# A fused sparse attention and gated convolution kernel: another order for its hand-scheduled operations

## The chip, the cores and the metric

The kernel runs on one core of one Trainium2 chip. The core has five engines that work through queues of their own: TensorE (PE; its weight loads are listed as PEld), VectorE (DVE), ScalarE (ACT), GpSimd (POOL) and SyncE (SP, which here only issues transfers). The metric is the device time of one execution in microseconds (us), lower is better.

## The reference

Four batches of eight heads, 768 positions, 64 wide. Attention keeps, for each query, only the six chunks of 32 keys with the highest upper bound; the result goes through a causal five-tap gate, a product with `w_val` and a product with `w_out`.

```python
ub = np.sum(np.maximum(q[..., None, :] * k_min, q[..., None, :] * k_max), axis=-1)
top_chunks = np.argsort(np.where(causal, ub, -1e9), axis=-1)[..., -6:]
scores = np.where(sel & (pos[:, None] >= pos[None, :]), scale * q @ k.T, -1e9)
attn = softmax(scores)
x = (attn @ v).transpose(0, 2, 1, 3).reshape(B, S, H * D)
gate = sigmoid(sum(conv_w[k] * xp[:, k:k + S, :] for k in range(5)))
out = (gate * (x @ w_val)) @ w_out
```

## The kernel before

The 32 heads are taken as 16 pairs, numbered 0 to 15; four pairs make a batch. `build` lists the operations, each with its engine and what it reads and writes; `emit_in_order` issues them in the order of the table `ORDER`. Each engine then works through its own operations in exactly that order and waits at the first whose inputs, buffer or PSUM bank is not ready. A name is a kind, a pair and indices; digits behind "=" are PSUM banks, of which there are eight, and a bank that an operation takes must have been read out by the users before it.

The kinds, for pair p:

- `Lk`, `Lq`, `Lv` (SP) load k, q and v. `KT`, `QT` (PE, L641) transpose them. `KE` (ACT, L648) and `QH` (ACT, L683) copy the transposes out, `QL` (DVE, L722) keeps the rounding rest of q. `KX` (DVE, L654) takes the maximum and minimum of each chunk of keys, and `KB`, `KS` (POOL, L664 to L679) turn these into operands.
- `CF`, `BD` (PE, L755, L766) make the bounds, `T8` and `CM` (DVE, L774, L781) select the chunks into `NS`. The mask has to be transposed to `QM`: by PE and DVE (`MT`, L791, and `ME`, L795) for pairs 0 to 9, by a DMA transpose (`MD`, SP, L797) for pairs 10 to 15.
- `S` (PE, L809 to L814) makes the scores, in six parts of two banks each, one bank for each head; the mask enters as a second product (L814). `E` (ACT, L818) is the exponential, `A` (POOL, L830) the causal cut, `AV` (PE, L839) the product with v, `RC` and `NR` (DVE, L845, L849) the division, into `ON`.
- `XT` transposes the result into `xT`: by PE and `XTE` (DVE, L871, L882), or by a DMA transpose (SP, L863) for pairs 8 to 14. `XH` (POOL, L890) copies the edge for the convolution. `CV` (PE, L903) is the gate for two pairs, `TH` (ACT, L908) its tanh.
- For each batch b, `VL` (PE, L918) multiplies with `w_val`, `GV` (DVE, L924) applies the gate, `OU` (PE, L932) multiplies with `w_out`, `OE` (ACT or DVE, L940, L942) copies out and `ST` (SP, L945) stores.

The weights come in small transfers: POOL issues `wval`(j, r), eight of them, and `wout`; SP then copies each finished pair of `wval` to the other half of the partitions (`wvd`j, L1026).

PE uses its array in three shapes: whole (128 rows, most kinds), in halves (64 rows, `S` and `VL`) and in quarters (32 rows, `CV`).

Of the kernel before, what the change touches and what calls it, by code (L numbers as in the profile page):

```python
# [126 lines left out]
S1.3=35 E1.13 E1.03 CF2=6 AL2 BD2.1 BD2.5 BD2.4 Lv0 VC0 QL3.1 A1.13 KX3.00 KX3.11 KX3.01 KB3.5 KB3.0
KB3.1 BD2.2 BD2.3 T82.2 T82.5 T82.1 T82.3 QH3.0 S1.1=07 E1.11 E1.01 Lq4.0 A1.01 S1.4=54 QL3.0 T82.4
CM2 AH3 E1.14 S1.0=31 E1.10 E1.00 E1.04 A0.15 Lv1 KS3 KB3.2 KB3.3 Lq5.0 KT4.1=7 KX4.11 AV0.05=2
AV0.03 AV0.02 A1.14 KT4.0=0 S1.2=64 E1.12 E1.02 MT2=1 AV0.01 AV0.14=3 AV0.15 KX4.00 KX4.10 KX4.01  # L130
KB4.5 KB3.4 ME2 QT4.1=5 AV0.04 AV0.00 RC0.0 AV0.13 AV0.10 AV0.11 QH4.1 NR0.0 KE4.1 KE4.0 Lk5.0
AV0.12 QT4.0=4 QH4.0 S2.3=61 E2.13 S2.2=27 E2.12 E2.03 AL3 CF3=0 BD3.5 BD3.4 BD3.2 BD3.1 KB4.0 KS4
# [12 lines left out]
XTE0 AV2.10 RC2.1 MT5=3 ME5 KT7.0=6 S4.1=07 E4.11 A3.04 A3.15 E4.01 S4.0=54 E4.00 E4.10 S5.3=32
NR2.1 A3.01 KX7.01 AH6 KX7.00 A3.05 AV3.02=1 A3.03 KB6.0 AV3.01 AV3.04 AV3.03 KB6.5 KS6 AV3.05 A3.14
AV3.00 wval31 wval01 E5.03 KT7.1=7 KX7.11 KX7.10 RC3.0 NR3.0 QT7.0=0 QH7.0 QL7.0 A4.05 A4.13 QT7.1=5
QH7.1 KE7.1 KE7.0 A3.13 AV3.14=4 AV3.15 Lv5 A4.14 XH1 KB6.1 KB6.2 KB6.4 KB6.3 A4.03 A4.04 A4.15
CF6=3 A4.01 BD6.3 QL7.1 BD6.1 AV3.10 AV3.11 AV3.13 E5.13 BD6.4 AV3.12 RC3.1 NR3.1 S5.1=17 E5.11 AH7
S5.5=06 E5.05 E5.15 BD6.2 BD6.5 E5.01 S5.4=25 E5.14 E5.04 dg00 T86.5 T86.1 T86.4 T86.3 KB7.0 S5.0=70  # L150
# [6 lines left out]
TH1.00 S6.4=32 TH1.10 TH1.11 E6.14 E6.04 XT4=0 XTE4 KT9.0=6 KX9.01 KX9.00 KT10.1=5 A5.13 A6.05
QT9.1=7 VC7 KB8.5 Lk12.0 QH9.1 MT7=4 ME7 QL9.1 KB8.0 A5.04 wval10 A5.11 QT9.0=0 QH9.0 QL9.0 XT3=2
XTE3 VC5 AV5.02=4 A5.01 TH1.01 KB8.1 A6.13 KE9.0 A6.03 KS8 AV5.04 Lv9 AV5.03 AV5.05 AV5.01 AV5.00
S7.5=37 E7.05 AL8 S7.3=10 E7.03 KX10.11 RC5.0 AL9 KX10.10 S7.1=62 E7.01 A6.11 KB8.2 KB8.3 AV5.14=3  # L160
AV5.12 AV5.15 E7.15 A6.14 wval20 AV5.13 AV5.11 E7.13 CF8=1 KB8.4 BD8.4 KE10.1 BD8.1 AV5.10 E7.11
NR5.0 A6.04 BD8.5 KB9.5 BD8.3 BD8.2 KB9.0 A7.01 A6.01 S7.2=67 E7.02 E7.12 T88.5 RC5.1 T88.3 T88.2
# [5 lines left out]
S8.3=72 E8.03 E8.13 E8.12 E8.10 A7.14 T89.4 T89.5 XT6=1 T89.3 T89.1 CM9 XTE6 XT5=5 XTE5 AV7.12=0
MT9=4 ME9 KB10.5 KT11.0=7 KX11.00 KX11.01 KT11.1=1 KS10 KE11.1 A7.05 A8.15 A8.14 A7.13 AV7.00=2
AV7.15 AV7.13 AV7.11 AV7.14 AV7.10 RC7.1 NR7.1 A7.04 AV7.02 AV7.05 KE11.0 KX11.11 KB10.1 KB10.2  # L170
AV7.04 dg11 KX11.10 AV7.03 AV7.01 RC7.0 NR7.0 KB10.4 S9.5=56 E9.05 E9.15 S9.3=43 S9.4=70 E9.03 E9.14
S9.1=56 E9.11 E9.13 CF10=4 KB10.3 BD10.3 VC8 A8.13 BD10.1 A8.11 BD10.2 BD10.4 BD10.5 E9.01 A9.15
AV8.14=1 E9.04 A8.03 T810.5 T810.2 dg13 KB11.0 KB11.5 KB11.1 AV8.13 AV8.11 AV8.12 A8.01 AV8.10
AV8.15 RC8.1 T810.3 Lq11.0 Lq12.0 QT11.1=0 QH11.1 T810.4 Lk13.0 Lv11 NR8.1 QL11.1 QT11.0=2 QH11.0
T810.1 KS11 A9.05 A9.13 A9.11 QL11.0 KT12.1=6 KE12.1 S9.2=35 E9.02 KX12.11 CM10 KX12.10 S9.0=71
E9.00 E9.12 E9.10 KT12.0=0 dg10 AL11 KX12.00 QT12.1=2 QH12.1 AH11 QL12.1 QT12.0=3 QH12.0 QL12.0
KE12.0 XH5 CV5.0=7456 CV5.1 TH5.11 TH5.00 TH5.01 TH5.10 A8.04 VC9 AV8.02=1 AV8.01 KB11.2 AV8.04
A8.05 KB11.3 KB11.4 XH3 CF11=2 BD11.4 A9.14 BD11.5 BD11.3 wvd2 wvd3 wvd0 MD10 S10.4=36 E10.14
KX12.01 T811.3 S10.5=07 BD11.2 T811.2 T811.5 AV8.05 E10.05 KB12.5 AV8.03 E10.04 S10.3=54 E10.03
# [918 lines left out]
```

## Time and profile before

| | |
|---|---|
| three runs, us | 183.22, 183.95, 182.49 (median 183.22) |
| profiled execution, us | 182.86, of it 181.2 span (first to last instruction) |
| busy, us | PE 175.2, PEld 127.3, ACT 140.4, DVE 123.3, POOL 109.1 |
| granted TensorE clock | 1.00 throughout |
| transfers | 29.68 MB, 28.06 MB of it on SP's queue |

A busy engine in the table counts each instruction from its start to its end, and the next may start before. Idle time and waits are named by what came last before the engine went on. A start in a timeline is in us from the start of the span.

### The profile page before, as it was taken

The page shows a single profiled execution, that of the slowest core. Times are in us where ns is not written, and L with a number is a line of the kernel's source. Part 1 is how long each engine was busy: PE and PEld are TensorE (multiplying, and loading weights), DVE is VectorE, ACT ScalarE, POOL GpSimd, SP SyncE. Part 2 cuts the span into 40 slices and gives each one's busy share as a digit, 9 for nine tenths or more (in the row PEclk, how much of TensorE's full clock was granted, in tenths as well). Part 3 has the DMA queues.
Part 4 walks back from the last instruction along what each step waited for, and adds up shares of the span by engine and source line. Part 5 has one row for each costly group of instructions (what it writes and reads, how often), then busy time and mean ns, then how long its engine had stood idle before and what let it go on. Part 6 is the DMA issues. An engine that isn't in the chain of part 4 may idle for free.

```text
span 181.2 us, 8892 instructions
## 1 busy us (share of the span) xinstructions
PE 175.2 (97%) x3714; PEld 127.3 (70%) x3714; DVE 123.3 (68%) x429; ACT 140.4 (78%) x320; POOL 109.1 (60%) x309
## 2 busy tenths in 40 slices
PE   7999999999999999999999999999999999999991
PEld 5896667868878687787866685687567678656541
DVE  0569999999999799998765679558925233611360
ACT  2279999999999999999897867595867979357032
POOL 6955898999999979899919633374551615000000
PEclk9999999999999999999999999999999999999999
DMA  5999999999999999980697995895226149337045
GB/s 99 224 220 215 213 201 236 213 211 227 210 222 190 219 191 189 183 175 10 135 164 150 207 206 117 176 95 149 43 47 103 60 117 231 96 108 289 7 183 222
DMA packets 89912, 29.68 MB, mean 164 GB/s; under 512 B 85387, under 2 KB 86667, under 8 KB 89872
## 3 DMA queue, kind: packets, MB, share of 16 engines
q1 hardware_dynamic: 88880, 28.06, 73.5%
q0 software_dynamic: 992, 1.06, 4.5%
q8 instruction: 29, 0.48, 1.2%
q14 instruction: 11, 0.09, 0.2%
HBM read 20.98 MB, written 6.29 MB: 151 GB/s over the span
## 4 chain that ended last, share of the span: by engine, by line
PE 91%; DVE 5%; issue 1%; POOL 0%; ACT 0%
PE ps L918 12%; PE ps L839 12%; PE ps L932 12%; PE ps L641 11%; PE ps L811 10%; PE ps L903 9%; PE ps L814 9%; PE ps L766 6%; PE ps L950 4%; DVE KK L654 2%; PE ps L871 2%; PE ps L791 2%; PE ps L809 2%; PE ps L714 1%; DVE ON L849 1%
## 5 line engine op out<-in xcount | busy, mean ns | idle before, releaser
L818 ACT ACTIVATE P<-ps 128x512 f16<-128x512 f32 (+1 forms) x192 | 90.2, 600 | 5.4 <-PE ps L814 4.8
L830 POOL TENSOR_SCALAR_AFFINE_SELECT P<-P 128x256 f16<-128x256 f16 (+1 forms) x128 | 43.1, 358 | 23.6 <-ACT P L818 21.9
L654 DVE TENSOR_REDUCE KK<-ps 128x12 f32<-128x384 f32 x64 | 32.8, 550 | 7.1 <-PE ps L641 6.5
L814 PE MATMUL ps<-QM,EM 64*128 64x512 f16 (+4 forms) x256 | 36.9, 290 | 0.2
L811 PE MATMUL ps<-QH,KE 64*128 64x512 f16 (+4 forms) x256 | 35.1, 291 | 0.0
L924 DVE SCALAR_TENSOR_TENSOR GV<-G,ps 128x384 f16<-128x384 f32 x32 | 16.4, 548 | 22.8 <-PE ps L918 22.1
L839 PEld LDWEIGHTS <-P 128*128 128x128 f16 x672 | 26.1, 98 | 6.3 <-issue 3.3
L839 PE MATMUL ps<-VA,P 128*128 128x65 f16 x672 | 30.3, 194 | 0.2 <-issue 0.2
L940 ACT ACTIVATE OSB<-ps 128x512 f32<-128x512 f32 (+1 forms) x22 | 12.9, 594 | 15.6 <-PE ps L932 8.4
L918 PE MATMUL ps<-xT,wv 64*128 64x384 f16 x256 | 23.3, 323 | 0.3 <-issue 0.3
L932 PE MATMUL ps<-wo,GV 128*128 128x512 f16 (+1 forms) x100 | 22.7, 370 | 0.0
L774 DVE MAX8 TOP<-ps 128x8 f32<-128x16 f32 (+4 forms) x160 | 15.9, 166 | 6.6 <-PE ps L766 5.1
L918 PEld LDWEIGHTS <-wv 64*128 64x128 f16 x256 | 13.1, 94 | 8.3 <-issue 1.2
L908 ACT ACTIVATE G<-ps 128x384 f32<-128x384 f32 x32 | 13.9, 498 | 6.6 <-PE ps L903 6.6
L811 PEld LDWEIGHTS <-KE 64*128 64x128 f16 x256 | 13.6, 94 | 6.2 <-issue 1.6
L849 DVE TENSOR_TENSOR ON<-ps,RCP 128x384 f16<-128x384 f32 x32 | 17.5, 552 | 0.7
L648 ACT ACTIVATE KE<-ps 128x384 f16<-128x384 f32 x32 | 17.0, 569 | 1.0 <-DVE RCP L845 0.7
L683 ACT ACTIVATE QH<-ps 128x384 f16<-128x384 f32 x32 | 16.0, 556 | 2.3 <-PE ps L641 2.2
L903 PE MATMUL ps<-xT,diag 32*32 32x384 f16 x1280 | 17.3, 326 | 0.0
L741 POOL CAST VA<-vn 128x768 f16<-128x768 f32 x16 | 14.6, 915 | 3.8 <-DMA vn<-in_v_dram 3.7
L641 PE MATMUL ps<-ident,kn 128*128 128x128 f32 x96 | 15.7, 284 | 0.0
L903 PEld LDWEIGHTS <-diag 32*32 32x32 f16 x1280 | 14.0, 87 | 2.5 <-ACT P L818 0.4
(75 smaller groups left out, 304.3 us busy)
## 6 DMA issues: line engine op xcount, KB each, us to landing
vn<-in_v_dram SPq DMA_DIRECT2D x16, 384.0 KB, 6.1
out_dram<-OSB SPq DMA_DIRECT2D x23, 256.0 KB, 2.9
kn<-in_k_dram SPq DMA_DIRECT2D x30, 192.0 KB, 5.0
qn<-in_q_dram SPq DMA_DIRECT2D x30, 192.0 KB, 4.8
wv<-in_moe_w_val_dram POOLq DMA_DIRECT2D x8, 64.0 KB, 4.5
wo<-in_moe_w_out_dram POOLq DMA_DIRECT2D x4, 128.0 KB, 5.3
wv<-wv SPq DMA_DIRECT2D x4, 128.0 KB, 5.1
qn<-in_q_dram SPq DMA_DIRECT2D x4, 96.0 KB, 3.1
```

Of the source, the lines that this page charges most:

```text
L641: nc.tensor.transpose(out=pt[:, tl * 128:(tl + 1) * 128], in_=t[:, 3 * w + tl, :], identity=ident)
L648: nc.scalar.activation(out=KE[p % 3][:, w * HB:(w + 1) * HB], in_=bank(gr, None), func=AF.Copy)
L654: nc.vector.tensor_reduce(out=KK[p % 2][:, mx, w * 12:(w + 1) * 12], in_=bank(gr, None).rearrange("p (c t) -> p c t", t=CH), axis=AX.X, op ...
L811: nc.tensor.matmul(out=pq[hh][:, col + a:col + n], lhsT=KE[p % 3][HP[hh], ks], rhs=QH[p % 3][HP[hh], q0 + a:q0 + n], start=True, stop=False)
L814: nc.tensor.matmul(out=pq[hh][:, col + a:col + n], lhsT=EM[HP[hh], ks], rhs=qm[HP[hh], q0 + a - 128:q0 + n - 128], start=False, stop=True)
L818: e.EX = lambda p, hh, bi, tot, gr: nc.scalar.activation(out=PT[hh, bi, p % 2][:, 0:tot], in_=bank(gr, None)[:, 0:tot], func=AF.Exp, scale ...
L830: nc.gpsimd.affine_select(out=ap, in_=ap, pattern=[[0, n], [1, 128]], compare_op=ALU.is_ge, fill=0.0, base=0, channel_multiplier=-1)
L839: nc.tensor.matmul(out=pav[:, qt, :], lhsT=PT[a, bi, p % 2][:, col:col + 128], rhs=VA[p % 3][:, hh, jt, :], start=(jt == 0), stop=(jt == qt))
L849: e.NR = lambda p, hh, gr: nc.vector.tensor_tensor(out=ON[(p // 2) % 2][:, 2 * (p % 2) + hh].rearrange("p t h d -> p h t d"), in0=bank(gr, ...
L903: nc.tensor.matmul(out=pc[i][os], lhsT=diag[rs, cp * NG + gi, j, :], rhs=x[rs, gi, :, a:a + 128], start=(j == 0), stop=(j == 2 * KSZ - 1), ...
L918: nc.tensor.matmul(out=pv[h], lhsT=wval_sb[HP[h], n, wc:wc + 255:2], rhs=xT[HP[h], (b % 2) * 2 + cp, gi, :, LD:LD + 128], start=(n == 0), ...
L932: nc.tensor.matmul(out=po[:, 0:z - a], lhsT=GVT[(b % 2) * NCT + et][:, s * 128:(s + 1) * 128], rhs=wout_sb[:, et, a:z], start=(et == 0), s ...
```

## The change

Only the table `ORDER` is other: the same 140 operations stand first, and after them the same operations as before stand in another order. 342 of PE's 564 operations have another place in PE's queue (by up to 25 places), 158 of ACT's 319, 223 of DVE's 347, and 254 of POOL's 294 (by up to 83 places). SP's queue is the same, row for row. Some operations take another PSUM bank. PE changes between the three shapes of its array 82 times in place of 79. The table has one line less, so that every line number behind it is lower by one.

```diff
-KE2.1 G8 S0.5=46 E0.05 KB1.0 KB1.5 KB1.1 KS1 KB1.2 KB1.3 S0.4=51 E0.14 E0.15 E0.04 Lq3.0 S0.3=27
+KE2.1 G8 S0.5=46 E0.05 KB1.0 KB1.5 KB1.1 KS1 KB1.2 KB1.3 S0.4=51 E0.14 E0.15 E0.04 dg01 KB1.4 dg03
...
-XT14 NR15.1 ST2.0 OE2.1 ST2.1 OE2.2 XT15=3 XTE15 CV13.0=0217 CV13.1 TH13.01 OU2.4=5 OE2.4 XH15
+TH13.11 OU2.3=3 OU2.4=5 OE2.3 OU1.3=6 OE1.3 OU1.4=4 OE1.4 NR14.0 XT14 XH15 CV15.0=1063 CV15.1
```

PE, pair 3, the score parts S3.4 and S3.1. `ps` are PSUM tiles, `VA` with `P` is an AV, `KB` with `RH` to `QL` a BD. Before, the first product of S3.1 (L809) follows S3.4 (L811, L814) directly:

```order
L811 MATMUL ps_1000<-QH_96,KE_86 128x512
L811 LDWEIGHTS KE_86
L811 MATMUL ps_1001<-QH_96,KE_86 128x512
L814 LDWEIGHTS EM
L814 MATMUL ps_1000<-QM_89,EM 128x512
L814 LDWEIGHTS EM
L814 MATMUL ps_1001<-QM_89,EM 128x512
L809 LDWEIGHTS KE_86
L809 MATMUL ps_1008<-QH_96,KE_86 128x192
```

Now two BD (six matmuls each, the last one shown) and two AV stand between them:

```order
L813 MATMUL ps_990<-QM_89,EM 128x512
...
L765 MATMUL ps_958<-KB_115,QL_99 128x48
...
L838 MATMUL ps_932<-VA_94,P_1_140 128x65
...
L765 MATMUL ps_958<-KB_115,QL_99 128x48
...
L838 MATMUL ps_932<-VA_94,P_1_140 128x65
...
L838 MATMUL ps_932<-VA_94,P_1_142 128x65
...
L808 MATMUL ps_1018<-QH_96,KE_86 128x192
```

Bounds of pair 4 (BD4.3, BD4.1) and products of pair 1 (AV1.10, AV1.11) have moved between the two score parts; PE changes its array's shape twice more here.

POOL, the transfers of `w_val` (`wv`). Before, wval31 and wval01 stand together, ahead of the first edge copy (XH1, the two copies of `xT`):

```order
L830 AFFINE_SELECT P_1_143<-P_1_143 128x128
L1023 DMA wv_66<-in_moe_w_val_dram 32x2x512 x2
L830 AFFINE_SELECT P_0_126<-P_0_126 128x128
L830 AFFINE_SELECT P_0_130<-P_0_130 128x256
L830 AFFINE_SELECT P_1_142<-P_1_142 128x256
L830 AFFINE_SELECT P_0_131<-P_0_131 128x128
L890 COPY xT<-xT 128x4x2x4
```

Now wval01 stands behind the second edge copy (XH5, the first two rows) and the four operations that follow it:

```order
L889 COPY xT<-xT 128x4x2x4
L889 COPY xT<-xT 64x4x4
L829 AFFINE_SELECT P_0_130<-P_0_130 128x256
L673 COPY KB_115<-KC_114 64x4x24
L829 AFFINE_SELECT P_0_132<-P_0_132 128x128
L829 AFFINE_SELECT P_0_125<-P_0_125 128x128
L1022 DMA wv_66<-in_moe_w_val_dram 32x2x512
```

wval01 has moved from among the cuts of pairs 3 and 4 to among those of pair 8; SP's queue still has wvd0, which copies what it brings, directly ahead of MD10.

DVE, the divisions (RC, NR) of pairs 14 and 15 and the copy XTE15. Before, both NR of pair 14 stand ahead of those of pair 15:

```order
L849 TENSOR_TENSOR ON_150<-ps_4844,RCP_147 128x2x3x64
L845 RECIPROCAL RCP_148<-ps_4892 128x6
L849 TENSOR_TENSOR ON_150<-ps_4830,RCP_147 128x2x3x64
L845 RECIPROCAL RCP_148<-ps_4858 128x6
L849 TENSOR_TENSOR ON_150<-ps_4858,RCP_148 128x2x3x64
L849 TENSOR_TENSOR ON_150<-ps_4892,RCP_148 128x2x3x64
L882 COPY xT<-ps_4968 128x6x128
```

Now NR14.0, the last one that the DMA transpose XT14 needs, stands behind XTE15:

```order
L848 TENSOR_TENSOR ON_150<-ps_4848,RCP_147 128x2x3x64
L844 RECIPROCAL RCP_148<-ps_4861 128x6
L848 TENSOR_TENSOR ON_150<-ps_4861,RCP_148 128x2x3x64
L844 RECIPROCAL RCP_147<-ps_4832 128x6
L844 RECIPROCAL RCP_148<-ps_4868 128x6
L848 TENSOR_TENSOR ON_150<-ps_4868,RCP_148 128x2x3x64
L881 COPY xT<-ps_4961 128x6x128
L848 TENSOR_TENSOR ON_150<-ps_4832,RCP_147 128x2x3x64
```

NR14.0 has moved behind three more operations of DVE, and XT14 with it.

## Rows read from the trace of the kernel before

**Rows 1.** Stretches: us, then busy us (instructions) by engine, clock, DMA share, GB/s.

```profile
40.00:60.00 20.00, 19.86 (x382) 15.77 (x381) 19.38 (x73) 19.94 (x48) 18.91 (x56) 1.00 1.13 213
60.00:80.00 20.00, 19.95 (x511) 16.20 (x513) 18.17 (x61) 19.39 (x44) 17.28 (x46) 1.00 1.02 197
80.00:100.00 20.00, 19.76 (x587) 14.12 (x580) 14.60 (x51) 17.98 (x43) 15.25 (x43) 1.00 0.59 117
100.00:120.00 20.00, 20.00 (x417) 14.20 (x413) 13.48 (x41) 14.53 (x34) 8.65 (x29) 1.00 0.82 169
```

**Rows 2.** The chain that ended last: start, us, what.

```profile
159.99 3.56 PE ps L932 x16
...
168.57 0.32 issue
```

**Rows 3.** Timeline of PE at a change of shape: start, us, engine, line, operation.

```profile
30.79 0.21 PE L766 MATMUL ps<-KB,QH 128*128 128x48 f16 x2
30.84 0.18 PE L766 MATMUL ps<-KB,QL 128*128 128x48 f16 x1
30.95 0.23 PE L811 MATMUL ps<-QH,KE 64*128 64x128 f16 x2
```

**Rows 4.** Timeline of PE, the two heads of S3.1.

```profile
36.47 0.24 PE L809 MATMUL ps<-QH,KE 64*128 64x192 f16 x1
...
36.71 0.24 PE L809 MATMUL ps<-QH,KE 64*128 64x192 f16 x1
```

**Rows 5.** Timelines of PE and DVE, 64.9 to 66.8 us: XT3, AV5, S7.1, XTE3.

```profile
64.91 0.50 PE L871 MATMUL ps<-identh,ON 128*128 128x128 f16 x6
65.45 0.84 PE L839 MATMUL ps<-VA,P 128*128 128x65 f16 x21
...
66.75 0.24 PE L809 MATMUL ps<-QH,KE 64*128 64x192 f16 x2
...
66.10 0.55 DVE L882 COPY xT<-ps 128x768 f16<-128x768 f16 x1
```

**Rows 6.** Issues on the page: median us from issue to landing at the end.

```profile
wv<-in_moe_w_val_dram POOLq DMA_DIRECT2D x8, 64.0 KB, 4.5
...
QM<-NS SPq DMA_TRANSPOSE x6, 2.6
```

**Rows 7.** Timelines of SP, DVE, POOL and PE, 76 to 90 us.

```profile
76.64 2.79 SPq L1026 DMA_DIRECT2D wv<-wv  x3
85.88 1.30 SPq L797 DMA_TRANSPOSE QM<-NS  x1
...
89.08 3.28 SPq L1026 DMA_DIRECT2D wv<-wv  x1
...
77.22 1.02 DVE L882 COPY xT<-ps 128x768 f16<-128x768 f16 x2
...
80.05 1.39 POOL L830 TENSOR_SCALAR_AFFINE_SELECT P<-P 128x256 f16<-128x256 f16 x4
...
89.19 0.39 PE L811 MATMUL ps<-QH,KE 64*128 64x512 f16 x2
```

**Rows 8.** Timelines of PE, DVE, SP and POOL, 155 to 164 us.

```profile
157.51 0.50 PE L871 MATMUL ps<-identh,ON 128*128 128x128 f16 x6
...
163.48 1.84 PE L903 MATMUL ps<-xT,diag 32*32 32x384 f16 x139
...
156.21 1.02 DVE L849 TENSOR_TENSOR ON<-ps,RCP 128x384 f16<-128x384 f32 x2
158.49 0.56 DVE L882 COPY xT<-ps 128x768 f16<-128x768 f16 x1 [1.25 <-PE ps L871]
...
155.79 1.39 SPq L863 DMA_TRANSPOSE xT<-ON  x1
...
159.16 0.46 POOL L890 COPY xT<-xT 128x32 f16<-128x32 f16 x2 [4.74 <-DVE xT L882]
```

**Rows 9.** The DMA transposes into xT, seven of them, all of the span.

```profile
DMA to landing us min/median/max: 2.7/3.6/7.5
```

More of the change, by code (lines that the diff above doesn't have):

```diff
@@ L127 @@
[L127 to L132, printed above, removed]
@@ L145 @@
[L145 to L150, printed above, removed]
@@ L157 @@
[L157 to L162, printed above, removed]
@@ L168 @@
[L168 to L173, printed above, removed]
@@ L174 @@
[L174 to L179, printed above, removed]
@@ new lines @@
+AL8 E6.02 E6.10 CV1.0=6517 CV1.1 TH1.00 TH1.10 A6.01 VC7 TH1.11 KB8.0 KS8 KB8.1 XT4=0 XTE4 S6.4=32
+E6.14 E6.04 A6.04 MT7=4 ME7 KT9.0=6 KX9.00 KX9.01 QT9.1=7 QH9.1 QL9.1 QT9.0=0 QH9.0 QL9.0 KT10.1=5
+TH1.01 AV5.04=4 AV5.03 A5.05 KB8.2 XT3=2 XTE3 A5.14 A6.13 A6.03 KB9.5 KB8.4 Lk12.0 Lv9 Lv8 Lq11.0
+Lq12.0 Lk13.0 AV5.02 AV5.01 AV5.05 KE9.0 KX10.10 KX10.11 AH9 KB8.3 Lv11 S7.5=37 E7.05 S7.3=10 E7.03
+S7.1=62 AV5.00 E7.01 A7.01 AV5.11=3 AV5.13 AV5.15 AV5.14 E7.13 CF8=1 BD8.3 BD8.5 AV5.10 BD8.4 AV5.12
@@ new lines @@
+E8.00 E8.10 dg13 A7.13 T89.5 T89.2 T89.3 T89.1 T89.4 CM9 S8.3=72 E8.13 wval11 XT6=1 XTE6 XT5=5 XTE5
+MT9=4 KB10.2 ME9 AV7.10=0 A7.14 AV7.15 KT11.0=1 KX11.01 KB10.4 KX11.00 E8.03 E8.12 KT11.1=3 KE11.1
+AV7.00=2 A8.01 VC8 XH5 KE11.0 AV7.11 AV7.12 AV7.03 AV7.01 AV7.14 AV7.13 RC7.1 NR7.1 AV7.05 AV7.02
+AV7.04 RC7.0 S9.5=56 E9.05 E9.15 S9.3=47 E9.03 S9.4=10 E9.04 A8.13 KB10.3 A8.15 A8.04 S9.1=56 E9.11
+E9.13 E9.01 CF10=4 AH10 BD10.1 wvd2 wvd3 wval01 KX11.11 BD10.2 BD10.5 BD10.3 NR7.0 KX11.10 BD10.4
@@ new lines @@
+T810.2 T810.4 T810.1 A8.11 A8.14 AV8.14=1 AV8.10 AV8.13 T810.3 T810.5 AV8.15 AV8.11 AV8.12 RC8.1
+E9.14 CM10 wvd0 MD10 NR8.1 A9.05 A8.03 KT12.1=6 KE12.1 KX12.11 QT11.0=2 QH11.0 QL11.0 S9.2=35 E9.12
+Lq13.0 QT11.1=0 QH11.1 KX12.10 QT12.0=7 wout3 S9.0=41 E9.02 KB11.0 KB11.5 KB11.1 E9.00 KT12.0=5
+KE12.0 E9.10 QH12.0 A9.04 QT12.1=2 QH12.1 QL11.1 AH11 dg10 XH3 AL11 CV5.0=6430 CV5.1 TH5.01 TH5.11
+A8.05 AV8.05=1 AV8.03 AV8.01 QL12.1 A9.15 KS11 KB11.2 KB11.3 QL12.0 KX12.01 A9.01 KB11.4 wout2
+KX12.00 TH5.00 CF11=2 BD11.5 VC9 AV8.02 BD11.4 BD11.2 T811.2 AV8.04 AV8.00 RC8.0 TH5.10 S10.5=07
@@ new lines @@
+GV2.11 S15.0=73 S15.5=14 E15.11 AV14.04=0 AV14.05 GV2.00 ST0.4 ST0.5 A14.11 AV14.10=6 AV14.01 GV2.01
+OU2.0=2 A15.01 E15.10 A15.14 AV15.12=5 AV14.02 AV15.00=3 A15.13 AV15.13 A14.13 AV14.14 E15.00
+AV15.02 AV14.11 AV14.00 AV14.12 A14.15 AV14.15 AV15.03 AV14.13 RC14.1 NR14.1 E15.05 E15.15 A15.15
+A15.11 AV15.10 AV15.15 AV15.04 A15.05 AV15.14 AV15.05 AV15.11 RC15.1 NR15.1 AV14.03 RC14.0 AV15.01
+RC15.0 NR15.0 OU2.2=4 OE2.2 OU2.1=6 OE2.1 XT15=3 XTE15 XH13 CV13.0=7154 CV13.1 TH13.10 TH13.01 OE2.0
+TH13.11 OU2.3=3 OU2.4=5 OE2.3 OU1.3=6 OE1.3 OU1.4=4 OE1.4 NR14.0 XT14 XH15 CV15.0=1063 CV15.1
```

150 lines of the change are left out of this document (79 added, 71 removed).

## The prediction

> **What bounds the kernel now.** I read the stretches first, then the chain, then the timelines of the places where the order moves something that is waited for.
>
> In the stretches [rows 1] the reader is to see two regimes. From 40 to 60 us ACT is busy 19.94 of 20 us, from 60 to 80 us 19.39: the exponentials and copies set the pace, and PE, though shown busy 19.86 and 19.95, spends part of it waiting inside an operation. From 100 us on PE is busy 20.00 of 20 and ACT only 14.53. Between the two, from 80 to 100 us, neither is full: PE 19.76, ACT 17.98.
>
> The chain that ended last shows what PE's 20.00 is worth late: sixteen matmuls of 512 columns take 3.56 us [rows 2], 0.22 us each, one behind the other at a granted clock of 1.00 [rows 1]. There is nothing to win by order there, only waits to be added. One loss in the chain has no releaser, 0.32 us of "issue" in the middle of a VL [rows 2]; no operand is named for it, so no order of operations owns it, and I leave it in.
>
> The Trainium skill ("Perfetto Trace Analysis", Identifying the Most-Contended Engine) warns that TensorE's matmul busy time is no measure of its headroom and asks to judge by the busy share of the weight loads. By that share, 14.20 of 20 us after 100 us [rows 1], an estimate would give PE some 30% of room and this change more to win; the spacing of the matmuls in rows 2 says that there is next to none, and the measurement decides.
>
> So the time can move in three ways: waits before 100 us that go or come, changes of the array's shape, and late waits that did not exist.
>
> **The change part by part.** The sum is made against the profiled execution, 182.86 us (181.2 of span and 1.66 around it), which is 0.36 below the median of the three runs, 183.22.
>
> 1. *ACT's stretch, 40 to 80 us.* The same ACT work is in front of each score part to within one or two instructions, so the order can win ACT's idle time and no more: 0.06 + 0.61 = 0.67 us [rows 1]. That is not quite a bound, since an ACTIVATE is counted to its end and short gaps don't show. The lower end is nothing. How much of a removed wait comes through is seen at one moved place: S3.1 starts its first head at 36.47 us and its second at 36.71 [rows 4], a wait of 0.24 us inside the operation, for its second bank. The new order puts two BD and two AV in front of it, which fills the wait, but it changes the array's shape twice more, and a change costs the step from 30.84 to 30.95 us less the usual step of 0.025 (two matmuls in 0.05) [rows 3]: 0.085 us. Of 0.24 us, 0.07 are left. The next score parts stay behind ACT. I take a little under half of 0.67: **-0.3 us**.
>
> 2. *MT7 and ME7, 65 us.* The six transposes of XT3 begin at 64.91 and are counted to 65.41 [rows 5]. A matmul of 48 columns is counted 0.18 us though the next starts 0.025 us behind it [rows 3], so AV5 could start some 0.16 us before that end, at 65.25; it starts at 65.45 [rows 5], 0.2 us later, held by the bank that ME7 reads. In the new order MT7 and ME7 stand some 1.3 us of PE's work ahead of AV5 (four transposing groups), and this wait goes. What is late next is S7.1, at 66.75 us: it takes the bank that XTE3 leaves at 66.10 + 0.55 = 66.65 [rows 5], and XTE3 has the same DVE work before it as it had. 0.1 us comes through, between 0 and 0.2: **-0.1 us**.
>
> 3. *80 to 100 us.* Neither engine is full, so between nothing and ACT's idle 2.02 us [rows 1] could be won. PE shows 0.24 us idle there, and the waits inside its operations are not in that figure. I stay near PE's row, 0.24 and half of another wait such as that in rows 4: **-0.36 us**.
>
> 4. *The array's shapes.* 82 changes in place of 79, at 0.09 us: **+0.27 us**. The Trainium skill ("TensorEngine Tiling (Array Packing)", Key Properties) says that a change of the tiling mode drains TensorE, which speaks against these three; it gives no price, and the sum goes by rows 3.
>
> 5. *The weights, SP and MD10.* wval01 moves behind XH5 on POOL. XH5 needs XTE5, the second of two copies that end at 77.22 + 1.02 = 78.24 us [rows 7]. Two copies (0.46 us, as in rows 8), three cuts at 1.39/4 = 0.35 us [rows 7] and a small KB come before it: wval01 goes out at about 80.0 us, lands 4.5 us later [rows 6], at 84.5, and only then can SP issue wvd0. Behind wvd0 in SP's queue waits MD10, and behind MD10 the first scores of pair 10, which start at 89.19 us [rows 7]. Three wvd take 2.79 us to issue, 0.93 each; one took 3.28 [rows 7]. MD10 then lands 2.6 us after its issue [rows 6]: 84.5 + 0.93 + 2.6 = 88.0 in the usual case, 84.5 + 3.28 + 2.6 = 90.4 in the bad one. Before, MD10 was issued at 85.88 and landed at about 88.5. So nothing, or up to 1.2 us. I take **0**: the price that three of four wvd paid.
>
> 6. *The tail.* XT14 needs NR14.0, which now stands behind XTE15. Before, XTE15 started at 158.49 us though XT15's transposes ended at 158.01; 158.49 is 155.79, XT14's issue, plus 2.7, the shortest landing of such a transpose [rows 8, 9], so I read it as having waited for XT14, whose turn now comes after. Then XTE15 runs from about 158.05 to 158.6, NR14.0 ends half of 1.02 us later, at 159.1, and XT14 goes out at 159.2. It lands at 161.9 if it takes 2.7 us, XH15 copies 0.46 [rows 8], and CV15 could start at 162.5. PE comes to CV15 at 163.48 [rows 8], with CV13 and four OU as cover. The cover holds by 1.0 us, that is up to a landing of 3.7 us. The median of the seven is 3.6, the longest 7.5 [rows 9]. Here no load is ahead of XT14 in SP's queue and the stores ahead of it went out long before, so I take the short one: **0**. The far end is the longest landing: 7.5 - 3.7 = 3.8 us.
>
> The moved cuts and KB operations on POOL are waited for by AV and BD. POOL is idle 1 to 5 us of each 20 here [rows 1], and a POOL operation that stands earlier than its input merely waits, with later ones behind it; I saw no place where PE arrives first, and cost them at nothing. If that cover were gone at a place, it would cost one cut, 0.35 us.
>
> Sum: -0.3 - 0.1 - 0.36 + 0.27 = -0.49 us. 182.86 - 0.49 is 182.4; the same step from the median of the runs is 182.7. I put down **182.6 us**.
>
> **The rivals.**
>
> *The order pays in full.* All of ACT's idle time from 40 to 100 us comes through (0.06 + 0.61 + 2.02), and ME7's 0.2, against 0.27 for the shapes: -2.6 us, 180.2 us at the most; two thirds of it, some 181.1, is the likely size. For it: gaps too short to show add to it, and hardly an engine row stays as it was. Against: at the two places priced above a third to a half of the wait is left.
>
> *SP holds up pair 10, and it is slower.* One mechanism, part 5 in its bad case: wvd0 leaves late and MD10 with it. At 3.28 us for wvd0 and a wval01 that is 1 us later than I reckon, the scores of pair 10 wait 2.2 us, and PE has only a few BD and AV to do meanwhile: 182.4 + 2.2 = 184.6 us. It decides against the change from the point where MD10 lands later than 89.7 us, which would eat the gain of 0.49; it is over 1% slower only if MD10 lands after 92 us, or if XT14 in the tail also takes over 6 us to land.
>
> *Nothing comes through.* ACT and PE are as full as before, and only the three changes of shape remain: 183.1 us, or 183.5 from the median.
>
> **How the numbers follow.** Chances: forecast 0.55, the full pay 0.17, nothing 0.16, SP or the tail 0.12. One per cent, 1.8 us, is about what a measurement of this kernel can tell from no change (its three runs lie 1.46 us apart). Faster by more than that, under 181.4 us, takes most of the second case and a little of the first: 0.17. Slower by more, over 185.05, takes the bad half of the last case and a little of what I have not seen: 0.09. The rest, 0.74, is within it. The range leaves out the lower half of the second case and the worst of the last: 181.1 to 184.6 us.
>
> **What would show it.** In the changed profile PE's stretch after 100 us stays at 20.00 of 20, and ACT from 40 to 80 us stays above 39.3 of 40. The two heads of S3.1 start together. AV5 follows the transposes of XT3 without a gap, and S7.1 waits for XTE3. MD10 is issued by about 86 us, right behind a wvd0 that waited for wval01. XTE15 follows XT15 at once, and XH15 ends before PE has done the last OU ahead of CV15. I am wrong if PE shows a gap ahead of the scores of pair 10 or ahead of CV15, or if the first score parts of pairs 5 to 9 start more than 1 us earlier than before, which would mean that ACT had more to give than its busy time shows.

## The result and the profile after

After takes 186.17 us (median of six runs, 185.11 to 186.60), before beside it 183.58 (six runs, 181.96 to 184.39): a ratio of 1.0148, 95% interval 1.0111 to 1.0185. It is slower, and above the range I gave. The profiled execution of after took 186.60 us (184.9 of span), that of before 182.86. Of the kernels below, four of a_mix's ten executions (187.0 to 188.2 us), one of b_w_a's four (193.43) and one of a_noload64's two (204.85) lie over 1.5% above the fastest of their kernel and are left out of the ratios, though not of the medians, and what slowed them is not shown.

The stretches of after, to be held against [rows 1] (columns as there):

```profile
40.00:60.00 20.00, 19.74 (x382) 15.95 (x381) 18.95 (x72) 19.97 (x48) 19.04 (x55) 1.00 1.06 210
60.00:80.00 20.00, 19.85 (x500) 15.91 (x497) 18.11 (x61) 19.02 (x44) 17.23 (x46) 1.00 1.04 189
80.00:100.00 20.00, 17.76 (x491) 13.06 (x487) 13.52 (x52) 15.81 (x38) 15.59 (x42) 0.91 0.80 108
100.00:120.00 20.00, 19.92 (x492) 14.62 (x473) 12.64 (x37) 12.87 (x29) 6.68 (x24) 1.00 0.84 145
```

Three of the four read as before. From 80 to 100 us PE is busy 17.76 where it was 19.76, ACT 15.81 where it was 17.98, and the clock is 0.91. The chain that ended last (start, us, what) tells where in that stretch:

```profile
86.74 1.43 PE ps L902 x108
88.17 0.48 issue
88.65 0.87 PE ps L902 x52
...
92.81 1.76 issue
94.57 0.38 PE ps L838 x7
```

Two gaps, both called "issue", the name for time in which an engine waits for nothing that the profile shows. The first stands inside the matmuls of one convolution (CV5.1), the second inside the products of one pair (between AV9.01 and AV9.02). Neither stands where an operand or a bank is waited for. Before's chain has one such row [rows 2], 0.32 us; after's two make 2.24.

The second gap is followed by a lower clock in this execution (stretches of 2 us of after, columns as above):

```profile
92.00:94.00 2.00, 0.81 (x18) 0.49 (x15) 1.24 (x10) 2.00 (x6) 2.00 (x6) 1.00 0.72 139
94.00:96.00 2.00, 1.43 (x32) 1.30 (x32) 0.98 (x3) 0.50 (x2) 1.22 (x4) 0.96 0.24 43
96.00:98.00 2.00, 2.00 (x20) 1.10 (x17) 1.10 (x3) 1.54 (x4) 0.37 (x2) 0.50 1.17 47
98.00:100.00 2.00, 2.00 (x92) 1.72 (x91) 1.24 (x4) 1.07 (x3) 1.90 (x4) 0.69 1.17 211
```

PE was busy 0.81 of 2 us and 1.43 of 2, and then worked at 0.50 (1.2 GHz) and 0.69. At full speed the same work would have needed up to 2 x 0.50 + 2 x 0.31 = 1.6 us less. 2.24 - 0.32 + 1.6 = 3.5 of the 3.74 us between the two profiled executions; the 1.6 is an estimate from these rows.

### The profile page after: what moved, and what is told of

Same layout as the page of the kernel before. It is cut to its first block, busy times and chain, and to the rows that moved or that the text cites. A ratio compares the mean times of both kernels' runs of the same rounds, so it can differ in the third digit from the quotient of the medians.

```text
span 184.9 us, 8905 instructions
## 1 busy us (share of the span) xinstructions
PE 176.8 (96%) x3714; PEld 129.7 (70%) x3714; DVE 123.6 (67%) x429; ACT 140.4 (76%) x320; POOL 109.5 (59%) x309
## 4 chain that ended last, share of the span: by engine, by line
PE 80%; ACT 14%; issue 3%; DVE 1%
PE ps L931 11%; PE ps L917 11%; ACT P L817 11%; PE ps L640 10%; PE ps L838 10%; PE ps L902 9%; PE ps L810 8%; PE ps L813 7%; PE ps L765 5%; PE ps L949 3%; ACT KE L647 2%; ACT QH L682 2%; PE ps L870 2%; PE ps L713 1%; PE ps L808 1%
## 5 line engine op out<-in xcount | busy, mean ns | idle before, releaser
L829 POOL TENSOR_SCALAR_AFFINE_SELECT P<-P 128x128 f16<-128x128 f16 (+1 forms) x128 | 43.2, 359 | 25.3 <-ACT P L817 23.8
L813 PE MATMUL ps<-QM,EM 64*128 64x64 f16 (+4 forms) x256 | 36.5, 293 | 0.0
L810 PE MATMUL ps<-QH,KE 64*128 64x64 f16 (+4 forms) x256 | 34.8, 294 | 0.5 <-ACT P L817 0.3
L838 PE MATMUL ps<-VA,P 128*128 128x65 f16 x672 | 31.3, 195 | 1.8 <-issue 1.8
L838 PEld LDWEIGHTS <-P 128*128 128x128 f16 x672 | 26.8, 99 | 6.7 <-issue 4.6
L773 DVE MAX8 TOP<-ps 128x8 f32<-128x24 f32 (+4 forms) x160 | 15.7, 166 | 6.4 <-PE ps L765 4.7
L917 PEld LDWEIGHTS <-wv 64*128 64x128 f16 x256 | 14.4, 94 | 6.7 <-issue 0.7
L721 DVE SCALAR_TENSOR_TENSOR QL<-ps,QH 128x256 f16<-128x256 f32 (+1 forms) x30 | 13.9, 481 | 2.8 <-ACT QH L682 2.8
```

The lines of the kernel that those rows point to most:

```text
L810: nc.tensor.matmul(out=pq[hh][:, col + a:col + n], lhsT=KE[p % 3][HP[hh], ks], rhs=QH[p % 3][HP[hh], q0 + a:q0 + n], start=True, stop=False)
L813: nc.tensor.matmul(out=pq[hh][:, col + a:col + n], lhsT=EM[HP[hh], ks], rhs=qm[HP[hh], q0 + a - 128:q0 + n - 128], start=False, stop=True)
L829: nc.gpsimd.affine_select(out=ap, in_=ap, pattern=[[0, n], [1, 128]], compare_op=ALU.is_ge, fill=0.0, base=0, channel_multiplier=-1)
L838: nc.tensor.matmul(out=pav[:, qt, :], lhsT=PT[a, bi, p % 2][:, col:col + 128], rhs=VA[p % 3][:, hh, jt, :], start=(jt == 0), stop=(jt == qt))
L917: nc.tensor.matmul(out=pv[h], lhsT=wval_sb[HP[h], n, wc:wc + 255:2], rhs=xT[HP[h], (b % 2) * 2 + cp, gi, :, LD:LD + 128], start=(n == 0), ...
```

## The experiments

**Theories.** Two lines of the page of after, the engines' busy time and instructions and the queue that brings PE its instructions (packets, MB, share):

```profile
PE 176.8 (96%) x3714; PEld 129.7 (70%) x3714; DVE 123.6 (67%) x429; ACT 140.4 (76%) x320; POOL 109.5 (59%) x309
...
q8 instruction: 29, 0.48, 1.2%
```

29 packets of 16 KB carry 3714 matmuls and as many weight loads: 7428 / 29 = 256 instructions, or 128 matmuls, to a packet. Counting matmuls from the start of the span shows what the two gaps have in common (stretches of after; the first number with x is PE's matmuls):

```profile
0.00:88.40 88.40, 86.01 (x1612) 66.53 (x1613) 74.72 (x278) 79.05 (x185) 74.54 (x208) 1.00 1.02 187
88.40:94.30 5.90, 4.16 (x128) 3.05 (x128) 3.65 (x17) 4.75 (x12) 4.67 (x12) 1.00 1.07 185
```

The first gap stands behind matmul 1612, the second 128 later, one packet, behind 1740. Both are 76 + 128 n. From this:

- T1: PE waits for its own instructions. They come in pieces of 128 matmuls. The next piece is asked for when a border (the place in PE's stream where one piece ends) is passed and must be there when the 128 are used up; a convolution uses 108 in 1.43 us (the chain above).
- T2: POOL's new order holds PE up. T3: the weight transfers that moved (wval01 from among pairs 3 and 4 to 81.6 us, wout3 to 83.4, wout2 to 88.9) are the reason, by what they are waited for or by being in front of the pieces. T4: the new order of PE and ACT costs it all, by its changes of shape and early waits.

**a_shift64, a_shift128, a_shift32, b_shift64: the same order, the instructions moved along.** The 36 fillers at the start (`FILL`, matmuls of 256 columns that nobody reads) are cut: the same columns in more matmuls. With n = 3 in 32 of them everything behind stands 64 matmuls later in PE's stream, with 2 it is 32, with 5 it is 128.

```diff
-        nc.tensor.matmul(out=pt[:, 0:256], lhsT=fz[:, 0:128], rhs=fz, start=True, stop=True)
+        n = 3 if len(done) <= 32 else 1
+        w = [256 * i // n for i in range(n + 1)]
+        for a, z in zip(w, w[1:]):
+            nc.tensor.matmul(out=pt[:, a:z], lhsT=fz[:, 0:128], rhs=fz[:, a:z], start=True, stop=True)
```

> After, with 32 of the filler matmuls of the first microseconds written as three matmuls of a third of the columns each: the same columns, the same order, but every later TensorE instruction stands 64 matmuls further on in its stream. Theory T1 (the unexplained gaps in after at 88 and 93 us are TensorE waiting for its own instructions, which come in pieces of 16 KB or 128 matmuls with their weight loads; the piece must be here before the last 128 matmuls are done): the borders of the pieces now fall so that each convolution (160 matmuls in about 2 us) runs through a whole piece; in after's trace six stretches of 128 matmuls between such borders last only 1.5 to 1.9 us (at 61, 87, 96, 115, 137 and 146 us), where a piece took 2.5 to 6 us to come. T1 expects 1 to 3.5 us more at each of them, 194 to 206 us in all, with the gaps inside CV. Theories T2 (POOL's new order holds TensorE up), T3 (the moved weight transfers as such) and T4 (the new order's array-shape changes and early waits) expect no change from after: 185.5 to 187.5.

> After, with 32 fillers written as five matmuls of a fifth of the columns each, so that every later TensorE instruction stands 128 matmuls further on: just one piece of 16 KB. T1: the borders fall on the same matmuls as in after, so the two gaps (0.8 us inside CV5, 1.8 us inside the pair 9 heads) stand where they were and the time is after's, 185.5 to 187.5; it is the control for the shift by 64. T2, T3, T4: no change either. A time far from after's would say that cutting up the fillers costs something by itself.

> After, with 32 fillers written as two matmuls of half the columns each: a shift by 32 matmuls, a quarter of a piece. T1: the stretches between borders around the convolutions now last 2.0 to 2.9 us by after's trace (they lasted 3.8 us and more without the shift, and 1.4 to 1.9 with the shift by 64), so the cost lies between: 190 to 196 us. All other theories: as after, 185.5 to 187.

> Before, shifted by 64 matmuls in the same way as after was. T1: the cost is a property of the stream and not of the new order: 195 to 203 us, gaps at matmuls 76 + 128 n inside or near the convolutions. If it were something in after's order that the shift laid open, before would stay at 183 to 185.

Measured: a_shift64 201.12 us (1.0957, interval 1.0886 to 1.1027), a_shift128 186.91 (1.0169, 1.0109 to 1.0229), a_shift32 195.25 (1.0655, 1.0583 to 1.0728), b_shift64 199.71 (1.0898, 1.0790 to 1.1006). Cutting fillers does nothing that data could wait for, and a whole piece of shift gives after's time again; half a piece costs 15 to 16 us in either order. In a_shift64's chain the gaps are these:

```profile
62.63 2.86 issue
94.53 1.61 issue
105.67 1.75 issue
125.91 1.03 issue
150.00 2.31 issue
161.05 1.65 issue
181.91 1.00 issue
```

and its stretches up to the first three of them:

```profile
0.00:65.30 65.30, 59.95 (x1105) 47.07 (x1105) 52.57 (x198) 54.43 (x128) 53.86 (x147) 1.00 1.00 201
65.30:96.00 30.70, 28.03 (x635) 21.79 (x636) 24.21 (x83) 26.53 (x61) 22.58 (x64) 0.94 0.73 138
96.00:107.20 11.20, 9.53 (x256) 6.53 (x255) 5.66 (x22) 6.54 (x14) 6.46 (x15) 0.85 0.48 86
```

1105, 1740 and 1996 are 1100 + 5, 1740 and 1996 of the series 76 + 128 n: the borders stayed and the operations moved over them. The seven gaps make 12.2 us; the clock, 0.94 and 0.85 in these stretches, takes more. T2, T3 and T4 expected 186 and fall as accounts of such gaps. Before can be made to lose as much as after, so the mechanism is not the new order's; what is left to tell is why the new order meets more of it. a_shift128's profile has its largest gap on the moved place of 1740 (1868), but only 0.67 us of it, and others of 0.4 to 0.5; its start is 0.9 us later (matmul 204, which is 76 of after, at 13.32 and 12.41 us) and PE waits 0.84 us for a transposed mask. That its time is after's is partly chance; what it shows is that cutting the fillers does not cost the 15 us.

The borders do not lie exactly at 76 + 128 n because PE's stream also holds semaphore waits, 53 in the trace of before, which take a place in a piece as matmuls and weight loads do. Counted with all that PE's queue lists, the 53 gaps of more than 0.25 us that the traces of this case (before, after and the seventeen runs here) call "issue" stand at instruction 192 to 194 + 256 n, and each ends 1.2 to 1.7 us after a packet of instructions has ended.

**What is in front of a piece.** At 83.33 us in before and 83.95 in after the same 1484 matmuls are done, a border of the series. In before hardly anything else is on the DMA engines (share 0.08 until 87.45), in after they are at 0.90:

```profile
0.00:83.33 83.33, 81.57 (x1484) 63.71 (x1485) 71.39 (x268) 74.47 (x175) 71.48 (x197) 1.00 1.05 198
83.33:87.45 4.12, 4.09 (x127) 2.74 (x125) 3.96 (x12) 4.12 (x11) 3.86 (x11) 1.00 0.08 18
```

```profile
0.00:83.95 83.95, 81.80 (x1484) 63.87 (x1484) 71.54 (x271) 74.72 (x176) 70.60 (x195) 1.00 1.02 192
83.95:88.60 4.65, 4.22 (x129) 2.67 (x129) 3.38 (x9) 4.32 (x11) 4.15 (x13) 1.00 0.90 94
```

The queues in after from 84.0 to 86.4 us (packets, MB, share), where no packet of instructions is among them:

```profile
q0 software_dynamic: 80, 0.13, 31.8%
q1 hardware_dynamic: 233, 0.15, 20.4%
```

From 86.4 to 87.4 us:

```profile
q8 instruction: 1, 0.02, 5.9%
```

From 88.7 to 91.7 us, again without one:

```profile
q1 hardware_dynamic: 2672, 0.68, 137.4%
```

From 91.7 to 93.1 us:

```profile
q0 software_dynamic: 75, 0.12, 47.7%
q8 instruction: 1, 0.02, 5.7%
```

And in before from 83.8 to 84.8 us, all that there is:

```profile
q8 instruction: 1, 0.02, 6.0%
```

The border is passed at 83.95 and no piece moves until 86.4, while POOL's wout3 (the 0.13 MB on q0) and 0.15 MB on SP's queue go through; the gap ends at 88.65. The next border is passed there, and no piece moves until 91.7, while 0.68 MB of loads go through in 2672 packets; that gap ends at 94.57, 5.9 us after the border. In before the piece asked for at 83.33 has moved by 84.8 us, alone. This is what the moved transfers could do. Four experiments try it.

**a_w_b and b_w_a: POOL's eleven weight transfers behind the POOL operations that they follow in the other order.** One line of each:

```diff
-Lq13.0 QT11.1=0 QH11.1 KX12.10 QT12.0=7 wout3 S9.0=41 E9.02 KB11.0 KB11.5 KB11.1 E9.00 KT12.0=5
+Lq13.0 QT11.1=0 QH11.1 KX12.10 QT12.0=7 S9.0=41 E9.02 KB11.0 KB11.5 KB11.1 E9.00 KT12.0=5
...
-AV3.00 wval31 wval01 E5.03 KT7.1=7 KX7.11 KX7.10 RC3.0 NR3.0 QT7.0=0 QH7.0 QL7.0 A4.05 A4.13 QT7.1=5
+AV3.00 E5.03 KT7.1=7 KX7.11 KX7.10 RC3.0 NR3.0 QT7.0=0 QH7.0 QL7.0 A4.05 A4.13 QT7.1=5
```

> After, with POOL's eleven weight transfers (wval, wout) issued behind the POOL operations that they followed in before; all other operations of all engines in after's order. T3 with T1 (the instruction piece waits behind these transfers, which in after move at 81 to 91 us: wval01, wout3, wvd0 and wout2): the gaps of 0.8 and 1.8 us at 88 and 93 us shrink to under 0.5 us together with the clock's drop behind them, 182.4 to 184.4. T2 or T4 (order of the computing operations): the gaps stay, 185.5 to 187.

> The mirror: before, with the eleven weight transfers behind the POOL operations that they follow in after. T3 with T1: TensorE's instruction pieces at 83 to 93 us come later, gaps of 0.5 to 2 us appear there at the borders of the pieces (before has 0.38 us at 91.6 and 0.35 us at 96.0), 184.5 to 187. T2 or T4: no change from before, 182.8 to 184.0.

Measured: a_w_b 186.02 us (1.0138, 1.0102 to 1.0173), nothing regained; b_w_a 192.13 (1.0437, 1.0375 to 1.0499), far more lost than expected, by another cause. In b_w_a's chain:

```profile
90.35 0.59 PE ps L766 x18
90.94 4.54 DMA QM<-NS
```

and on SP's timeline:

```profile
90.24 0.59 SPq L1026 DMA_DIRECT2D wv<-wv  x1
90.94 1.39 SPq L797 DMA_TRANSPOSE QM<-NS  x1
```

wval01 stands too late there for before's other operations, wvd0 waits for it, MD10 goes out at 90.94 instead of 85.88 [rows 7], and PE stands 4.2 us in front of pair 10's scores. It is the prediction's rival on SP, in a kernel that is not the changed one. In a_w_b the gap inside CV5 is gone and the one behind matmul 1740 shrinks to 0.94 us, but the transfers now stand where POOL has no room, and PE waits 1.2 us for POOL between 50 and 74 us (KB twice, until 58.2 us in its chain, and VA once); that the two sides cancel is argued, and the run decides nothing alone.

**a_wout_late and b_wout_a: only wout1 to wout3.** In a_wout_late the three stand at about 100 us; in b_wout_a they stand in before where after has them.

```diff
-A10.01 VC10 AL12 VL0.0=72 GV0.01 VC11 KS12 S11.2=43 TH3.00 S11.0=06 E11.00 E11.10 VL0.1=12 GV0.11
+A10.01 VC10 AL12 VL0.0=72 GV0.01 VC11 wout3 wout2 wout1 KS12 S11.2=43 TH3.00 S11.0=06 E11.00 E11.10 VL0.1=12 GV0.11
```

> After, with three of POOL's weight transfers (wout3, wout2, wout1; issued at 83.4, 88.9 and 94.6 us in after) put behind pair 11's copy of v, at about 100 us, where POOL waits most of the time; they are needed by the output products at 113 us. T1 with T3 (the instruction pieces of 84 to 93 us came late because these transfers went through ahead of them: 2048-byte packets from 85.3 to 86.4 us, then a piece at 86.4): the gap of 0.5 us inside CV5 goes, the one of 1.8 us among the pair 9 heads falls below 1 us, and with the clock that stays up the time is 183.0 to 184.8. T1 without T3 (the pieces come late because of the loads of the next pairs and of the transposed mask, not these): 185.3 to 186.8. T2, T4: 185.5 to 186.8.

> Before, with the same three transfers behind the POOL operations that they follow in after (about 83, 89 and 92 us), and wval and all else as in before, so that SP's queue is not held up. T1 with T3: the pieces of 84 to 93 us come later, one or two gaps of 0.5 to 2 us at matmuls 1612 and 1740: 184.3 to 186.3. T1 without T3, T2, T4: no change, 183.0 to 184.3.

Measured: a_wout_late 185.28 us (1.0137, 1.0069 to 1.0204), b_wout_a 183.72 (1.0015, 0.9980 to 1.0051). In a_wout_late the gap inside CV5 is gone, as T1 with T3 said, and that behind 1740 is 0.4 us; but 0.8 us now stand behind matmul 1104 (at 66.8 us) and 0.9 behind 1994 (102.4 us), both near a border. b_wout_a, before's order word for word up to 70 us, has a gap of 0.67 us behind matmul 1105 that before's profile does not have. These three transfers alone are not the cause; pieces are late wherever much is on the way, and which border is hit changes.

**ab_84, ba_84, ba_100, ab_60: halves.** One order up to a named operation, the other for what is left (ab: after's first; the number is the time in us of the seam). The seam of ab_84:

```diff
-E9.14 CM10 wvd0 MD10 NR8.1 A9.05 A8.03 KT12.1=6 KE12.1 KX12.11 QT11.0=2 QH11.0 QL11.0 S9.2=35 E9.12
+AV8.12 RC8.1 E9.14 CM10 wout3 wout1 dg11 A9.15 A8.03 KB11.0 KB11.5 KB11.1 QT11.1=0 QH11.1 NR8.1 QL11.1
```

> After's order of all engines up to and with CM10 (about 84 us), and from there on before's order of what is left. T1 in its wider form (TensorE's instruction pieces come late at borders that are run through fast; after's order of 84 to 100 us, with the moved transfers of POOL and SP, makes more of these gaps): the early half costs what after's trace shows at CV5, 0.5 to 0.8 us, and the rest is before's: 183.6 to 184.8. T4 (it is the early order: the array-shape changes and the waits of 20 to 80 us, whose cost only comes to light later): 185.3 to 186.6.

> The mirror: before's order up to and with CM10, then after's. T1: the gaps of after at 88 and 93 us come again, 185.0 to 186.4. T4: 183.0 to 184.3.

> Before's order up to and with AL12 (about 100 us), then after's: only the last part of the new order. All theories that put the loss ahead of 100 us: 182.9 to 184.2. After's trace shows 0.6 us lost between VL0 and CV15 and 0.4 us won in the tail, so a loss of the late part would give 184.5 or more.

> After's order up to and with CM6 (about 54 us), then before's: only the first part of the new order. After's trace is 0.3 us late there (S5), so T1: 183.5 to 184.3. T4: half or more of the loss, 184.8 to 186.

Measured: ab_84 186.12 us (1.0173, 1.0129 to 1.0218), ab_60 185.19 (1.0131, 1.0086 to 1.0177), ba_84 184.34 (1.0070, 1.0034 to 1.0107), ba_100 183.85 (1.0045, 1.0007 to 1.0084). By its numbers this is T4, not what I expected of T1: the early half alone carries the loss of after. Most of what ab_84's trace shows is T1's all the same. Its counts:

```profile
0.00:66.90 66.90, 63.55 (x1104) 48.33 (x1104) 55.48 (x205) 58.13 (x137) 55.31 (x153) 1.00 1.06 205
66.90:84.60 17.70, 17.04 (x374) 13.86 (x374) 15.85 (x66) 16.41 (x38) 14.91 (x42) 1.00 0.74 134
84.60:90.60 6.00, 4.88 (x134) 3.51 (x135) 5.31 (x12) 4.65 (x11) 5.77 (x15) 1.00 0.86 160
```

and what its matmuls waited for (line; total, times, longest):

```profile
PE ps L899 <- issue: 1.1, 1, 1.1
PE ps L835 <- issue: 1.0, 2, 0.8
PE ps L637 <- ACT P L814: 0.7, 1, 0.7
```

Gaps without a releaser stand behind matmuls 1104, 4 beyond the border 1100, and 1612 (1104 + 374 + 134), and 0.25 us behind 1740. The 0.7 us behind 1478 (1104 + 374) are not T1's, though 1484 is near: these are transposes that ACT releases, at the seam. I had tied T1 to the two gaps of one execution; the early order meets it at earlier borders when the late one is before's. The other halves say less: ab_60's profile, the fastest of its four executions (184.12 us), has 0.7 us of such gaps and 0.7 in which PE waits for POOL's KB behind the seam, and ba_84's has none over 0.25 and waits 1.0 us for DVE's NS. The 184.34 us of ba_84 miss both ranges, T1's by more, and a seam seems to cost waits of its own.

**a_noload, b_noload, a_noload64: the loads taken away.** The loads of q, k and v of pairs 7 to 15 are not issued; weights, masks and stores stay.

```diff
         en = nc.sync if eng == "SP" else nc.scalar
+        if p >= 7:
+            return
```

> After, without the loads of q, k and v of pairs 7 to 15 (the pairs are computed from what pairs 3 to 6 left in the same buffers, so the output is that of other inputs); the weight transfers, the transposed masks and the stores stay. T1 with the transfers as the reason for the lateness: the pieces land 0.5 to 2.5 us after their border is entered, no gap over 0.4 us at matmuls 1100, 1612 and 1740, and the time is 181.5 to 183.3, within 0.7 us of b_noload. T1 without the transfers (a piece is late for another reason): the gaps stay, 185 to 187. T4 (the order itself): 184 or more, some 2 us above b_noload.

> Before, without the same loads. T1: its few gaps (0.2 to 0.35 us by the profile, a little more on average) go, 181.5 to 183.0. T4 and the others: as before or up to 1 us faster.

> After without those loads and with the shift by 64 matmuls (201.1 us with the loads). T1 with the transfers: a piece still takes over a microsecond to come, so the stretches of 1.4 to 1.9 us still wait, but 0.5 to 1.2 us each instead of 1.0 to 2.9: 188 to 194. T1 without the transfers: 198 to 202.

Measured: a_noload 182.92 us (twelve runs, 182.55 to 183.37; 0.9970 of before, 0.9945 to 0.9996), b_noload 184.34 (183.79 to 184.75; 1.0054, 1.0032 to 1.0077), a_noload64 201.83 (two runs, 198.82 and 204.85; no ratio). After's loss is gone, and its order is now the faster one, for a reason given below. The list of waits of a_noload has no row in which PE's matmuls wait for "issue". After's six executions lie 1.5 us apart, the twelve without loads 0.8.

Two expectations failed. b_noload has a gap that before has not, in the chain

```profile
157.59 1.61 PE ps L905 x126
159.21 1.30 issue
```

inside CV13, 4 matmuls beyond the border 3404; before has its piece there in time (one packet between 154 and 157 us, where b_noload has none until 157). The traces have a lead. Without the waits for the loads PE's stream holds 34 semaphore waits in place of 53, and by the count above the border before this one has moved from matmul 3271, ahead of a semaphore wait of PE at 157.29 us in before, to 3280, behind the same wait (156.88 in b_noload). The piece starts at 155.47 in before and at 157.85 in b_noload, as if it were asked for only once that wait is over; no run tries it. It also means that leaving out the loads changes not the traffic alone: it moves borders, by up to 10 matmuls. At 84 and 88 us it is 5 and 6, and the pieces there start to move at 83.75 and 88.85 us in a_noload, where after's did at 86.44 and 91.80. And the shift by 64 costs as much without loads as with them: a_noload64's profiled execution takes 198.82 us, 15.9 more than a_noload's, and its seven gaps are 1.5 to 2.3 us each, 12.6 together. So the lateness has two parts. A piece takes some 3 to 4 us even without these loads (an estimate: a stretch of 128 convolution matmuls, 1.43 x 128 / 108 = 1.7 us, and the gap of 1.5 to 2.3 behind it), and up to 5.9 with loads in front. Worked out from the same rows, a border costs time if the 128 matmuls behind it take less than that.

**a_mix: all work kept, the new transfers cleared away; after_2: after once more.**

```diff
-A5.04 VC5 wval31 RC4.0 T87.3 NR4.0 QT8.1=2 QH8.1 QL8.1 A5.11 wout0 QT8.0=6 QH8.0 S6.1=41 E6.11 E6.01
+A5.04 VC5 wval31 wval11 wval01 RC4.0 T87.3 NR4.0 QT8.1=2 QH8.1 QL8.1 A5.11 wout0 QT8.0=6 QH8.0 S6.1=41 E6.11 E6.01
```

(wval11 and wval01 leave their places at 77 and 82 us; wout3, wout2, wout1 as in a_wout_late.)

> After, with wval11 and wval01 issued right behind wval31 (about 60 us; 77.0 and 81.6 in after), so that the copy wvd0 and the transposed mask MD10 behind it on SP's queue no longer wait for wval01 and go before TensorE enters the border at 84 us, and with wout3, wout2, wout1 at about 100 us as in a_wout_late. T1 with the transfers: the pieces for matmuls 1612 and 1740 land no later than 2.5 and 3.3 us after the border before them is entered (3.4 and 4.4 in after), gaps under 0.4 us there; 183.0 to 184.8 if nothing turns up elsewhere, 184.8 to 185.8 if the pieces of 62 or 96 us come late instead, as in a_wout_late. No influence of the transfers: as after, 185.5 to 186.8.

> After once more, word for word, for a second profile. T1: the time is 185.1 to 186.7 again, the gaps stand at matmuls 76 + 128 n again, but their places and sizes differ from the first profile (0.5 us at 1612 and 1.8 us at 1740 there), since the lateness of a piece is the chance of what is on its way. If the gaps were fixed by the order of the operations, they would be those two again, within 0.2 us.

Measured: a_mix 185.19 us (median of ten; ratio 1.0044, 0.9999 to 1.0090), after_2 186.49 (1.0162, 1.0076 to 1.0247). In a_mix the gap inside CV5 is gone and the one behind 1740 is 0.6 us instead of 1.8; 0.5 us stand behind 1104. Some two thirds of the loss are regained in the ratio, about half by the medians (185.19 and 183.76 beside it), and it does not beat before. The stretches of after_2:

```profile
0.00:62.20 62.20, 59.37 (x977) 45.23 (x977) 51.61 (x197) 54.36 (x128) 52.20 (x144) 1.00 1.07 202
62.20:89.00 26.80, 26.24 (x635) 20.70 (x636) 23.17 (x82) 24.69 (x57) 22.25 (x65) 1.00 0.84 147
89.00:95.00 6.00, 4.16 (x128) 3.05 (x128) 3.59 (x17) 4.85 (x12) 4.59 (x12) 1.00 1.06 182
```

and its waits, as for ab_84:

```profile
PE ps L838 <- issue: 1.8, 1, 1.8
PE ps L902 <- issue: 1.4, 2, 0.8
```

The two gaps of after are there again, behind 1612 and 1740 and of like size (1.8 again, 0.6), against what I expected: they belong to after's order with its transfers. A third, 0.8 us behind 977 (border 972), is new, and the clock stayed at 1.00 from 92 to 100 us; the execution took 186.67 us with the one and 186.60 with the other.

## Why the prediction was wrong

The step that failed is the one on the chain's loss without a releaser, 0.32 us of "issue": "no operand is named for it, so no order of operations owns it, and I leave it in." It was one of a kind. It stands behind matmul 3654, 6 short of the border 3660 (192 + 256 n with the semaphore waits), it ends 1.33 us after a packet of instructions, and it is PE waiting for instructions. An order owns such a loss in two ways: it sets which operations lie across a border, and by the places of the transfers what is on the DMA engines when the next piece is asked for. In the same way "cost them at nothing", of POOL's moves, left out the transfers among them: wout3 stood in front of a piece at 84 us, and the gap behind it was 0.48 us. Where wout3 stood elsewhere (a_w_b, a_wout_late, a_mix) that gap was gone; but in a_noload and b_wout_a wout3 stood at after's place and the gap did not come, so it takes more than this transfer.

The other steps:

- *Parts 1, 2 and 4, ACT's stretch, MT7 and the shapes, -0.13 together.* The sign was wrong, by up to half a microsecond. Without loads 1484 matmuls are done at 83.70 us in after's order and at 83.20 in before's: +0.5. Of it 0.2 stand at matmul 120 already (16.45 and 16.25 us), where both orders are still the same, so some +0.3 is the order's; 0.28 is one wait at 22 us, outside the stretches that I priced, in which PE waits for an exponential of ACT and which only after's order has. S3.1's two heads do start together, 37.27 us for both, and ACT's 40 us fell to 19.97 + 19.02 = 38.99, under the 39.3 that I gave as the mark; without the loads it is 19.97 + 19.26 = 39.23, so by this comparison the order takes 0.1 of it and the late pieces the rest. AV5 follows XT3 without the wait in a_noload (0.33 us from start to start, 0.54 in before); in after it began 0.57 us behind, at 66.24, on a border and 1.28 us after a packet of instructions: a late piece took the wait's place.
- *Part 3, 80 to 100 us, -0.36.* Right in size once the gaps are away: 1996 matmuls are done at 100.33 in a_noload and 100.25 in b_noload, so 0.42 of the 0.5 is won back there. In after the stretch lost some 3 us instead.
- *Part 5, SP and MD10, 0.* Right. wvd0 left at 83.99 and MD10 at 84.68 us, and no wait for QM follows. I was near the edge, as b_w_a shows: 5 us later costs PE 4.2 us.
- *Part 6, the tail, 0.* Right by less than I thought. XT14 went out at 163.68 us, XH15 copied from 167.02 for 0.46, and CV15 began at 167.65: 0.2 us of cover, not 1.0. XTE15 began 0.45 us behind the end of XT15's transposes again (162.50 and 162.05), so in before it had not waited for XT14, as I had read it.

All in all the order itself is worth about nothing: without loads, and without b_noload's 1.3 us gap, the two profiled executions are 182.93 and 183.87 - 1.30 = 182.57 us (by the medians 182.92 and 184.34 - 1.30 = 183.04). I had -0.49. The forecast of a time within one per cent would have stood but for the pieces.

The question could have been asked blind: before's page has the same 29 packets and 3714 matmuls, and its row of "issue" [rows 2] stands between two matmuls of one product.

Open: why the pieces of 62 to 67 us come later with after's early order (ab_84, ab_60, a_wout_late, a_mix) than in before's profile, when b_wout_a shows that before's order can meet it too; and whether b_noload's late piece has the reason given above. Whether POOL's computing operations have a part (T2) was not tried alone: PE waits for POOL in a_w_b and ab_60, up to 0.7 us at once, and after's profile has no such wait. And no run regains the whole loss with all the work kept.

## What to carry to other kernels

When a chain has a gap that nothing releases, in the middle of like instructions, count the instructions up to it, semaphore waits too: if such gaps stand multiples of a fixed number apart and end soon after a packet of instructions, the engine is waiting for its own instruction stream, and any edit that moves its instructions or the DMA traffic can move the cost. A long stream of short matmuls is fast work only where its piece is already there; a shift of the whole stream by a quarter and by half a piece, with dummy instructions, is a cheap test; here it cost 6 and 9 to 10 per cent. A sum that has no such term, as the one above, sees none of this, so small gains of an order are to be measured. It looks worth trying to keep transfers away from the borders that are passed fast, though a_mix regained only a part that way.
